# Token order restored at the eviction of y, token blocks outermost in its tile, and a new order of all compute steps, in a fused gated-recurrence and bilinear-FFN kernel

## The chip, the cores and the metric

The kernel runs on one core of a Trainium2 chip. The metric is the device time of one execution in microseconds (us), lower being better. Times are given as the median of several runs; the profile is of one execution, and its span reaches from that execution's first instruction to its last. The engines are named as the profile names them: PE (matmuls; PEld is its loading of weights), DVE (vector engine), ACT (scalar engine), POOL (GpSimd) and SP (which here only issues DMAs). POOL issues DMAs too. A source line of the kernel is written L919.

## The reference

Four batches, eight heads, 768 tokens, head dimension 48 (all inputs are float32). A gated linear-attention recurrence runs over the tokens, its output is laid out as 3072 tokens of 384 features, and a bilinear feed-forward network follows.

```python
def _attn_ref(q, k, v, alpha):
    B, H, S, D = q.shape
    state = np.zeros((B, H, D, D), dtype=np.float32)
    y = np.zeros_like(q)
    for t in range(S):
        state = alpha[:, :, t, :, None] * state + np.einsum('bhd,bhe->bhde', k[:, :, t], v[:, :, t])
        y[:, :, t] = np.einsum('bhd,bhde->bhe', q[:, :, t], state)
    return y

def _moe_ref(x, w_a, w_b, w_out):        # x (3072, 384), w_a and w_b (384, 1536), w_out (1536, 384)
    return (x @ w_a) * (x @ w_b) @ w_out
```

## The kernel before

**Tiling.** The work is cut into six chunks. Chunk c takes 256 consecutive tokens (number c//2 of the three such pieces of the sequence) of two batches (0 and 1 for even c, 2 and 3 for odd c); its two batches are called u = 0 and 1. The state of the recurrence passes from chunk c to chunk c+2. A load puts token pairs on the 128 partitions: partition p of `a`, `k`, `q`, `v` holds tokens 2p and 2p+1 of the 256, told apart by an index r. Partitions 0 to 63 and 64 to 127 are two blocks of 128 tokens each, called g = 0 and 1. So within a block the kernel's own order of columns is (r, s): the 64 even tokens, then the 64 odd ones. A block pair (u, g) makes four token blocks of 128 in a chunk, numbered 2u + g.

**Recurrence part of a chunk.** ACT takes logarithms of alpha (step `ln`, L556). Sums of pairs (`l2` on DVE, `l2s` on POOL) and triangular matmuls on PE (`B`, `A2`, `AQ`) give cumulative logs, and ACT exponentiates them (`E`, L667). DVE multiplies k and q by those factors into the tile `QKp` (`mk`, `mq`, L678). The scaled k and q are transposed into `kqT`, in chunks 0 and 1 by PE (`C`, L736) with copies out of PSUM (`Ce`), in later chunks by a DMA transpose that SP issues (`T`, L767). `dr` and `dl` (SP's DMAs through DRAM) or `dk` and `de` (PE and ACT) bring the decay factors of the state to where they are needed. `v` (L785 on ACT, L787 on DVE) casts v. `K`/`K2` are the state's matmuls on PE, `k` the state update on DVE. `D` (L841) computes scores k·q per head on PE in tiles of 64x64. They are masked either by DVE in one step (`M`, L846), or copied by ACT (`Mc`, L850) and then multiplied in place by DVE (`Mm`, L854). y is summed in PSUM from the part carried by the state (`SB`, `SA`) and the part within the block (`Y`; all three record L865).

**y's eviction.** `X u e` copies the 768 columns of both blocks of a batch from PSUM into `xT`, the transposed input of the network, on engine e (S: ACT, L900; V: DVE, L902). There are 12. `xT` is `[128, KT, B, C]`: on 128 partitions the three feature tiles, and in each the four token blocks of 128 columns. The columns keep the order (r, s).

**Network part of a chunk.** `a f w bank` and `b f w bank` (L919) multiply `xT` by 128 columns (feature block f of 12) of w_a or w_b: three matmuls that add up in one PSUM bank. With w = `*` they take all four token blocks (512 columns), with w = 0 or 1 the two blocks of one batch (256 columns). ACT copies a to SBUF (`as`, L925), DVE multiplies it by b, in PSUM, into `prod` (`pr`, L933). This product puts the tokens in natural order: it writes through `tokens`, which steps over every second element, and reads through `columns`. `o m half bank` (L941) does six of the twelve output matmuls of one token block (384 columns each), `oc` (L952) the same for half the columns in the last block of the last chunk; `ot`/`otc` (L956 on ACT, L958 on DVE) evict them, and `st`/`stc` store them by DMA (`Y` after a `st` or `ld` is SP, `P` is POOL).

**Weights.** `W a lo hi` and `W b lo hi` (L529) load columns lo to hi of w_a and w_b, `Wo` (L532) loads w_out, all issued by POOL between its other work, as are most loads of chunks 0 to 2.

**The order.** Nothing is reordered by a scheduler. A string, `PROGRAM` (lines 17 to 401), lists every step of every chunk in the order in which it is issued, chunk number first; a table `OPS` maps a step's name to a function. Each engine takes its own steps in that order, and semaphores hold a step until its operands are there and its buffer or PSUM bank is free. The last number of `a`, `b`, `o`, `D`, `SB` and the like is one of eight PSUM banks (`D` and `SB` take two). So the place of a step in the string sets what stands ahead of it in its engine's queue. In the list, chunks overlap: the recurrence steps of chunk c+1 stand among the network steps of chunk c.

Of the kernel before, what the change touches and what calls it, by code (L numbers as in the profile page):

```python
# [130 lines left out]
2: mq 0 V
1: b 3 1 3; b 0 0 6; as 3 1; as 0 0; b 0 1 7; pr 3 1; a 8 0 1; a 9 0 5
0: st 1 Y
1: b 8 0 3; b 9 0 4; pr 0 0; as 0 1
2: mk 0 V
1: a 4 1 2
3: ln *
1: a 9 1 6; pr 0 1; as 8 0; b 9 1 1
3: ra 1
1: b 10 1 7; pr 8 0; a 10 1 3; as 4 1; as 9 0; as 9 1; a 6 1 6; b 6 1 2; b 11 1 5; pr 4 1; as 10 1; pr 9 0; a 11 1 4; pr 10 1; pr 9 1; as 6 1  # L140
2: v 1 S
1: a 8 1 3; b 8 1 1; a 7 1 6; pr 6 1
3: l2 0 V
1: as 11 1
2: T 0
1: as 8 1; a 5 1 4
3: ra 0
1: as 5 1; a 1 1 2
2: v 0 V
4: ld a * Y  # L150
1: pr 11 1; as 7 1; pr 8 1
2: K2 * * 0 7; D 1 1 3; D 1 0 5
1: as 1 1; b 5 1 2; o 2 0 1
2: k * 0 V
1: pr 5 1
3: v 0 S; v 1 S
1: b 1 1 2
2: Mc 1 0; M 1 1
3: l2s 0 P; l2s 1 P
1: b 7 1 0; o 2 1 -; pr 1 1; o 3 0 4  # L160
2: SB 0 5
1: pr 7 1
3: R 0
2: D 0 0 2
1: ot 2 V
2: Mm 1 0 V
# [12 lines left out]
2: Y 1; SA 1; Mm 0 1 V; Mm 0 0 V; Y 0; X 0 S
3: E 0 b  # L180
4: l2 0 V
2: X 1 V
1: o 0 1 -
2: b 1 * 6; a 1 * 5
3: E 1 b
4: ld k * Y
3: E 1 i
1: ot 0 S
3: E 0 i
4: l2s 0 P  # L190
2: a 0 * 0; b 0 * 1; as 0 *; as 1 *
3: lv 0 k P; lv 0 q P
2: a 5 * 7
1: st 3 Y
2: a 7 * 4
4: l2s 1 P
2: a 2 * 5
3: lv 1 q V; mq 1 V; lv 1 k V
2: pr 1 *
3: dr  # L200
2: pr 0 *
3: mk 0 V
4: ld q * Y
0: st 2 Y
2: as 5 *; a 6 * 6; b 6 * 2; as 7 *
3: mq 0 V
2: b 9 * 4; b 7 * 0
1: st 2 Y
3: dl
4: R 0  # L210
2: b 5 * 7
1: o 1 0 3
2: a 9 * 1; pr 7 *; as 6 *
3: T 0
2: pr 6 *
4: ra 0
2: pr 5 *; a 11 * 6
3: mk 1 V
2: as 9 *; a 3 * 0
4: lv 0 k V; lv 0 q V; R 1  # L220
2: as 2 *
1: o 1 1 -
2: as 11 *; a 8 * 5; b 11 * 2; a 4 * 7; b 2 * 1
3: T 1
1: ot 1 V
2: pr 9 *; as 8 *; pr 11 *; pr 2 *; b 8 * 3; b 4 * 5; as 4 *
# [872 lines left out]
```

## Time and profile before

| | |
|---|---|
| time, median of 3 runs | 194.18 us (193.73 to 194.41) |
| span of the profiled execution | 192.0 us (its whole time is not recorded apart from the span) |
| `a` and `b` matmuls, L919 | 540, busy 112.0 us |
| output matmuls, L941 | 276, busy 49.4 us |
| score matmuls, L841, and y's, L865 | 384 and 576, busy 9.0 and 10.5 us |
| products, L933, on DVE | 90 |
| y evictions, L900 and L902 | 9 on ACT and 3 on DVE, busy 7.2 and 2.9 us |
| DMA | 29.40 MB, 153 GB/s on average |
| granted TensorE clock | 1.000 |

A row such as "L919 ... x270 | 56.0, 337" gives a group of instructions, their number, their busy time in all and the mean duration of one in ns. Matmuls are pipelined, so their durations overlap, and the mean of one is longer than the time by which each moves the next: with 512 columns they follow each other in less than the 337 ns that the mean shows. In the row of slices, PE is busy at 90% or more in all but the first and the last of the 40 slices of 4.8 us:

```profile
PE   7999999999999999999999999999999999999992
DVE  2387698994989888899897956887567446252510
ACT  4448885656779867753487756743572435314211
PEclk9999999999999999999999999999999999999999
GB/s 132 274 219 218 251 253 235 244 269 264 251 107 166 165 216 265 248 254 149 233 213 181 156 174 129 3 42 140 146 66 44 85 0 0 0 0 3 164 82 82
```

DVE and ACT are busiest in the first two thirds, where recurrence and network steps overlap, and little in the last fifth. The transfers are over, but for the last stores, by about 154 us.

### The profile page before, as it was taken

The numbers are of one execution on the slowest core, as the hardware profiler recorded it, in microseconds if no ns is written. First come the engines' busy times: TensorE is split into PE (matmuls) and PEld (weight loads), VectorE is DVE, ScalarE is ACT, GpSimd is POOL, SyncE is SP. The second block draws the span as 40 slices with busy tenths as digits, with TensorE's granted clock in tenths as the row PEclk, the third lists the DMA queues.
The fourth block names the chain that finished last, engine by engine and source line by source line (L and its number), as shares of the span: only waits on it lengthen the run. The fifth ranks groups of instructions, "written<-read, shape, count | busy, mean of one in ns | idle before, by whom it ended". The sixth has DMA issues, their size and how long they took to land.

```text
span 192.0 us, 6086 instructions
## 1 busy us (share of the span) xinstructions
PE 186.8 (97%) x2613; PEld 116.9 (61%) x2613; DVE 133.1 (69%) x223; ACT 106.5 (55%) x194; POOL 56.9 (30%) x75
## 2 busy tenths in 40 slices
PE   7999999999999999999999999999999999999992
PEld 3888875677778876645557444656465644545562
DVE  2387698994989888899897956887567446252510
ACT  4448885656779867753487756743572435314211
POOL 8999626752450500640074262000000000000000
PEclk9999999999999999999999999999999999999999
DMA  5999999999969999999999989017641200000422
GB/s 132 274 219 218 251 253 235 244 269 264 251 107 166 165 216 265 248 254 149 233 213 181 156 174 129 3 42 140 146 66 44 85 0 0 0 0 3 164 82 82
DMA packets 62618, 29.40 MB, mean 153 GB/s; under 512 B 53712, under 2 KB 60768, under 8 KB 62592
## 3 DMA queue, kind: packets, MB, share of 16 engines
q0 software_dynamic: 18432, 13.37, 39.6%
q1 hardware_dynamic: 44016, 15.55, 38.1%
q8 instruction: 20, 0.33, 0.7%
q10 hardware_dynamic: 144, 0.10, 0.2%
q14 instruction: 6, 0.05, 0.1%
HBM read 25.98 MB, written 4.74 MB: 160 GB/s over the span
## 4 chain that ended last, share of the span: by engine, by line
PE 91%; DMA 5%; SPq 1%; DVE 1%; issue 1%; ACT 0%; DVEq 0%
PE psum L919 47%; PE psum L941 24%; PE psum L865 7%; PE psum L841 3%; DMA kqT<-QKp 3%; DMA q_t<-in_q_dram 3%; PE psum L736 2%; PE psum L633 1%; PE psum L952 1%; SPq L549 1%; PE psum L799 1%; PE psum L812 1%; PE psum L700 1%; PE psum L591 1%; PE psum L592 1%
## 5 line engine op out<-in xcount | busy, mean ns | idle before, releaser
L919 PE MATMUL psum<-xT,wb_t 128*128 128x512 bf16 (+1 forms) x270 | 56.0, 337 | 0.0
L919 PE MATMUL psum<-xT,wa_t 128*128 128x512 bf16 (+1 forms) x270 | 56.0, 337 | 0.0
L941 PE MATMUL psum<-wo_t,prod 128*128 128x384 bf16 x276 | 49.4, 326 | 0.0
L919 PEld LDWEIGHTS <-wb_t 128*128 128x128 bf16 x270 | 25.9, 98 | 19.9 <-issue 0.5
L919 PEld LDWEIGHTS <-wa_t 128*128 128x128 bf16 x270 | 25.9, 98 | 19.7 <-issue 0.3
L941 PEld LDWEIGHTS <-prod 128*128 128x128 bf16 x276 | 25.9, 98 | 17.6
L956 ACT ACTIVATE ot<-psum 128x384 f32<-128x384 f32 (+1 forms) x16 | 7.7, 482 | 22.7 <-PE psum L941 21.6
L850 ACT ACTIVATE m<-psum 128x1024 bf16<-128x1024 f32 x14 | 14.1, 1023 | 4.6 <-PE psum L841 4.3
L613 POOL TENSOR_TENSOR l<-la 64x384 f32<-64x384 f32 x7 | 7.8, 1108 | 26.6 <-ACT la L556 19.0
L846 DVE TENSOR_TENSOR m<-psum,mask 128x1024 bf16<-128x1024 f32 x10 | 12.1, 1220 | 3.1 <-PE psum L841 3.1
L652 POOL TENSOR_TENSOR q_t<-q_t,ra 128x384 f32<-128x384 f32 x5 | 6.1, 1215 | 22.5 <-ACT ra L645 19.7
L556 ACT ACTIVATE la<-a_t 128x1536 f32<-128x1536 f32 (+2 forms) x9 | 9.5, 1055 | 2.3 <-DMA a_t<-in_alpha_dram 2.2
L678 DVE TENSOR_TENSOR QKp<-q_t,beta 128x768 bf16<-128x768 f32 x10 | 10.0, 995 | 1.0 <-ACT beta L667 1.0
L865 PE MATMUL psum<-m,vx 64*64 64x128 bf16 x576 | 10.5, 217 | 0.0
L900 ACT ACTIVATE xT<-psum 128x768 bf16<-128x768 f32 x9 | 7.2, 816 | 5.7 <-PE psum L865 5.5
L678 DVE TENSOR_TENSOR QKp<-k_t,invb 128x768 bf16<-128x768 f32 x10 | 9.7, 972 | 0.8 <-ACT invb L667 0.8
L854 DVE TENSOR_TENSOR m<-m,mask 128x1024 bf16<-128x1024 bf16 x14 | 9.3, 684 | 1.2 <-ACT m L850 1.2
L958 DVE COPY ot<-psum 128x384 f32<-128x384 f32 (+1 forms) x9 | 4.8, 532 | 7.6 <-PE psum L941 4.7
L865 PEld LDWEIGHTS <-vx 64*64 64x64 bf16 x576 | 9.0, 107 | 0.5 <-issue 0.3
L841 PE MATMUL psum<-kqT 64*64 64x128 bf16 x384 | 9.0, 219 | 0.4 <-DMA kqT<-QKp 0.3
L652 POOL TENSOR_TENSOR k_t<-k_t,a_t 128x384 f32<-128x384 f32 x6 | 7.4, 1228 | 6.1 <-issue 3.3
L549 POOL DMA_DIRECT2D v_t<-in_v_dram x8 | 8.5, 1058 | 0.1
(271 smaller groups left out, 287.9 us busy)
## 6 DMA issues: line engine op xcount, KB each, us to landing
out_dram<-ot SPq DMA_DIRECT2D x23, 192.0 KB, 3.8
q_t<-in_q_dram SPq DMA_DIRECT2D x3, 768.0 KB, 6.5
a_t<-in_alpha_dram POOLq DMA_DIRECT2D x2, 768.0 KB, 15.2
k_t<-in_k_dram POOLq DMA_DIRECT2D x2, 768.0 KB, 12.1
v_t<-in_v_dram POOLq DMA_DIRECT2D x4, 384.0 KB, 7.0
a_t<-in_alpha_dram SPq DMA_DIRECT2D x2, 768.0 KB
k_t<-in_k_dram SPq DMA_DIRECT2D x2, 768.0 KB
a_t<-in_alpha_dram POOLq DMA_DIRECT2D x3, 384.0 KB, 8.5
```

The costliest lines, as they stand in the source:

```text
L549: eng.dma_start(out=t[:, us, hs].rearrange("p b h r d -> p (b h) (r d)"), in_=src[ch.b0 + us.start:ch.b0 + us.stop, hs, ch.s * 2 * C:(ch.s ...
L556: nc.scalar.activation(out=ch.la[:, us, hs].rearrange("p b h r d -> p (b h r d)"), in_=ch.a[:, us, hs].rearrange("p b h r d -> p (b h r d) ...
L613: eng.tensor_add(ch.l2[(1 - g) * HC:(2 - g) * HC, 1], x[:, :, 0, :], x[:, :, 1, :])
L652: eng.tensor_mul(x, x, by)
L678: eng.tensor_mul(QKp[ch.c % 2][:, u, j, :, hs, :D], src[:, u, hs].rearrange("p h r d -> p r h d"), f)
L841: nc.tensor.matmul(s2[g * HC:(g + 1) * HC, r, p, rk, :], lhsT=turned_part(ch, u, 1, rk, 2 * h + p, g, rs), rhs=queriesT(ch, u, 2 * h + p, ...
L846: nc.vector.tensor_mul(m.rearrange("p r a k s -> p (r a) (k s)"), ch.s2[u, h].rearrange("p r a k s -> p (r a) (k s)"), maskn(4))
L850: nc.scalar.activation(out=m.rearrange("p r a k s -> p (r a) (k s)"), in_=ch.s2[u, h].rearrange("p r a k s -> p (r a) (k s)"), func=AF.Copy)
L854: eng.tensor_mul(x, x, maskn(4))
L865: nc.tensor.matmul(y[c * DP:(c + 1) * DP, g, j // 2 * C:(j // 2 + 1) * C], lhsT=lhsT, rhs=rhs, start=(g, c) not in begun, stop=False, skip ...
L919: nc.tensor.matmul(p, lhsT=(wa_t, wb_t)[w][:, kk, f * 128:(f + 1) * 128], rhs=ch.xT[:, kk, us, :], start=(kk == 0), stop=(kk == KT - 1))
L941: nc.tensor.matmul(op, lhsT=ch.prod[:, f, at:at + C], rhs=wo_t[:, f, :], start=(f == 0), stop=(f == NFF - 1))
```

## The change

`xT` becomes `[128, B, KT, C]`: token blocks outermost, the three feature tiles within. `X u e` becomes `X u g e`: one block (384 columns) is evicted at a time, so there are 24 evictions instead of 12, of half the size each. 17 are on ACT and 7 on DVE. The eviction now writes the columns in natural token order: its output steps over every second element. So `pr` reads and writes plain runs, and the helpers `tokens` and `columns` are gone. A matmul `a` or `b` reads, for feature tile kk, one run of 128 columns out of each token block, 384 columns apart, where it read one run of 512 or 256.

The string `PROGRAM` is replaced. The steps are the same in kind, number and width (90 `a`, 90 `b`, 46 `o`, 4 `oc`), but for `X`. All compute steps stand in new places, with new PSUM banks. POOL's steps stand in the same sequence, and so do the loads that SP issues; SP's stores and its `dr`, `dl` and `T` have moved among those loads in places. Four `v` casts move from ACT to DVE, and three `ot` evictions move from ACT to DVE. The first program lines (up to the first network steps), the places where chunk 4's logarithms and chunk 2's masking stand, and the end are shown in full below; the rest of the string is left out.

```diff
 PROGRAM = """
-0: cm 0; c1; cz 0 b P; ci; ld a 0b Y; c1a; ld a 0a Y; ln 0b; cu; cz 1 b P; fill 7 2; cu2 V; cz 0 q V; cus; ld k 0b Y; ld k 0a Y; B 0b 5; ld q 0b Y; ld v 0 P
-0: ln 0a; ld q 0a Y; E 0b b; E 0b i; mq 0b V; B 0a 0; E 0a i; dk 0 2; E 0a b; ld a 1 P; mk 0b V; C 0 1 5; cs 0 m P; ld k 1 P; ld q 1 P; v 0 S; mk 0a V; cm 1
-0: de 0; fill 2 1; mq 0a V; C 0 0 3; Ce 0 1 V; W b 0 256; cz 0 v P; Ce 0 0 V; D 0 1 4; ln 1; ld v 1 P; W a 256 768; K 0 0 6; k 0 0 V; M 0 1; D 0 0 0; SB 0 6
-0: cz 1 q P; B 1a 2; M 0 0; W a 0 256; E 1a i; E 1a b; W b 256 768; mq 1a V; mk 1a V; B 1b 4; dk 1 3; E 1b i; E 1b b; de 1; v 1 S; mq 1b V; mk 1b V; C 1 0 0
-0: Y 0; SA 0; Ce 1 0 V; cs 1 m P
-1: ld a 0 P; ld a 1 P
-0: W a 768 1536; C 1 1 1; X 0 S; c2 P; D 1 0 3; W b 768 1536
-1: ld q 0 P
-0: Ce 1 1 V; K 1 0 5; k 1 0 V; a 4 0 0
-1: ld k 0 P
-0: D 1 1 6; SB 1 1
-1: ld v 0 P; ld q 1 P
-0: Mc 1 0; a 3 0 5; Wo 0 6; a 0 0 3; Mm 1 0 V; Mc 1 1; as 0 0; b 0 0 4
-1: ld k 1 P
-0: pr 0 0; b 1 0 6; a 2 0 3; a 1 0 7; a 5 0 4; as 2 0; b 2 0 3; Mm 1 1 V; as 1 0; b 4 0 7; as 5 0; b 5 0 4; pr 2 0; pr 1 0
-1: ln 0
-0: SA 1; Y 1; Wo 6 12; K 1 1 6; as 3 0; as 4 0; X 1 S
...
+0: ld a 0b Y; c1a; c1; cm 0; ld a 0a Y; cz 0 b P; fill 7 0; ln 0b; ci; cu; cu2 V; cus; ln 0a; B 0b 2; cz 1 b P; ld k 0b Y; B 0a 0; dk 0 4
+0: ld k 0a Y; E 0b i; mk 0b V; ld q 0b Y; cz 0 q V; ld v 0 P; E 0b b; mq 0b V; C 0 1 5; fill 2 2; ld q 0a Y; E 0a b; mq 0a V; E 0a i; mk 0a V; ld a 1 P; C 0 0 0; v 0 V
+0: K 0 0 1; cs 0 m P; ld k 1 P; Ce 0 0 V; Ce 0 1 S; de 0; D 0 1 2; ld q 1 P; k 0 0 V; D 0 0 4; cm 1; M 0 1; W b 0 256; M 0 0; SB 0 0; ln 1; B 1a 6; E 1a i
+0: B 1b 2; dk 1 4; cz 0 v P; mk 1a V; E 1a b; mq 1a V; C 1 0 5; ld v 1 P; E 1b i; mk 1b V; E 1b b; de 1; W a 256 768; Y 0; SA 0; X 0 1 S; cz 1 q P; mq 1b V
+0: C 1 1 4; X 0 0 S; Ce 1 0 V; D 1 0 2; Mc 1 0; v 1 V; K 1 0 5; K 0 1 1; Ce 1 1 V; D 1 1 6; k 1 0 V; SB 1 4; W a 0 256; a 1 0 0; as 1 0; a 3 0 2; k 0 1 V; b 1 0 3
+0: pr 1 0; as 3 0; Mm 1 0 V; W b 256 768; a 0 0 0; b 3 0 1; Mc 1 1; Mm 1 1 V; cs 1 m P; pr 3 0; as 0 0; b 4 0 2; b 5 0 3; a 5 0 0; as 5 0; a 2 0 6; K 1 1 7; k 1 1 V
+0: Y 1
+1: ld a 0 P
+0: SA 1; X 1 0 V; a 4 0 0; b 0 0 1
...
+0: X 1 1 S; b 2 1 4
+1: ln 1; l2 1 V
+0: b 3 1 1; as 4 0; pr 4 0; a 2 1 5
 1: H 1 V
...
+0: as 2 1; pr 2 1; a 3 1 0; as 3 1; pr 3 1; W a 768 1536; a 7 * 3; as 2 0; a 6 * 0; a 9 * 2; c2 P; as 9 *; a 1 1 6; b 5 1 1; W b 768 1536
+1: ra 0; A2 0 4; E 0 i; E 0 b; L 1 V
+0: pr 2 0; b 9 * 2; pr 9 *; a 5 1 7
...
-2: Mc 0 1
-4: ln *
...
+4: ln *
+3: R 0
+2: Mc 0 1
+0: cs 0 0 P
+1: o 3 0 1; o 3 1 -
+3: R 1; AQ 6; E 1 b; E 1 i; E 0 b
+2: SA 0
...
-5: ot 0 V; o 2 1 -; oc 1 0 1 -; otc 1 0 V; ot 3 S; oc 1 1 0 0; st 0 Y; st 3 Y; ot 2 S; st 2 Y; oc 1 1 1 -; otc 1 1 S; stc 1 1 S; stc 1 0 Y
+5: o 0 0 0; pr 6 *; pr 8 *; o 3 0 1; o 3 1 -; o 2 0 2; o 2 1 -; ot 3 V; ot 2 V; o 0 1 -; ot 0 S; st 0 Y; st 3 Y; st 2 Y; oc 1 1 0 1; oc 1 1 1 -; otc 1 1 V; stc 1 1 S
+5: oc 1 0 0 0; oc 1 0 1 -; otc 1 0 S; stc 1 0 Y
 """
...
-    def evac(ch, u, eng):
+    def evac(ch, u, g, eng):
         if not hasattr(ch, "xT"):
-            ch.xT = wk.tile([128, KT, B, C], BF16, name="xT")
-        o_ = ch.xT[:, :, 2 * u:2 * u + 2, :].rearrange("p a g s -> p g a s")
-        i_ = ch.y[u][0][:, :, :KT * C].rearrange("p g (a s) -> p g a s", a=KT)
-        if eng is nc.scalar:
-            nc.scalar.activation(out=o_, in_=i_, func=AF.Copy)
-        else:
-            eng.tensor_copy(o_, i_)
+            ch.xT = wk.tile([128, B, KT, C], BF16, name="xT")
+        evict(ch.xT[:, 2 * u + g].rearrange("p a (s r) -> p a r s", r=2),
+              ch.y[u][0][:, g, :KT * C].rearrange("p (a r s) -> p a r s", a=KT, r=2), eng)
...
-    def tokens(x, us):
-        return x.rearrange("p (b s r) -> p b r s", s=HC, r=2)[:, us]
-
-    def columns(x, n):
-        return x.rearrange("p (b r s) -> p b r s", r=2, s=HC)
...
-            nc.tensor.matmul(p, lhsT=(wa_t, wb_t)[w][:, kk, f * 128:(f + 1) * 128], rhs=ch.xT[:, kk, us, :], start=(kk == 0), stop=(kk == KT - 1))
+            nc.tensor.matmul(p, lhsT=(wa_t, wb_t)[w][:, kk, f * 128:(f + 1) * 128], rhs=ch.xT[:, us, kk, :], start=(kk == 0), stop=(kk == KT - 1))
...
-        o_, a_, b_ = tokens(ch.prod[:, f, :], us), columns(a[:, :n], n), columns(b, n)
-        nc.vector.tensor_mul(o_, a_, b_)
+        nc.vector.tensor_mul(ch.prod[:, f, us.start * C:us.stop * C], a[:, :n], b)
...
-        "X": lambda x, u, e: evac(x, int(u), ENG[e]),
+        "X": lambda x, u, g, e: evac(x, int(u), int(g), ENG[e]),
```

`evict`, which the new `evac` calls, is the function that output evictions use already: on ACT an activation with the copy function, on DVE a copy.

More of the change, by code (lines that the diff above doesn't have):

```diff
@@ new lines @@
+2: K2 * * 5 3; D 0 0 6
+1: pr 9 1
+2: k * 0 V
+3: ld q * Y
+1: o 2 0 0
+3: l2 0 V
+1: b 6 1 1; b 4 1 2
+2: Mc 0 0; k * 1 V
+1: a 10 1 5; b 10 1 6
+3: ld k * Y
+1: a 6 1 7; o 2 1 -; as 4 1; pr 4 1
+3: v 0 S
+2: SB 0 2
+1: as 10 1; pr 10 1; as 6 1; pr 6 1
+3: l2s 1 P
+2: SB 1 4; D 0 1 6
+4: ln *
[5 more added lines that the diff above has]
+2: SA 0
+4: ld k * Y
+3: E 0 i
+2: Mm 0 1 V; Mm 0 0 V; Y 0; Y 1; SA 1; X 1 1 S
+1: o 0 0 7; o 0 1 -
+2: X 0 0 V
+0: st 1 Y
@@ new lines @@
+3: SA 1
+4: E 0 b; E 0 i
+1: st 0 Y
+4: E 1 i
+3: Mm 0 0 V; Y 0; Mm 1 1 V; Y 1; X 1 1 S; SA 0; X 0 1 S
+2: o 3 0 1; o 1 0 3
+3: X 1 0 S; X 0 0 V; b 8 * 2; a 3 * 4; a 1 * 5; a 8 * 6
+5: l2s 1 V
+4: lv 0 q V; mk 0 V; ld v * P; v 0 S
+3: as 8 *; a 9 * 7
+2: o 1 1 -
+4: mq 0 V; T 0
+5: ld k * P; l2 0 V; l2s 0 P; R 0; ra 0
+4: mk 1 V
+3: pr 8 *; as 1 *; as 3 *
+2: o 3 1 -
+3: b 1 * 2; pr 1 *
+2: ot 2 S; st 2 Y
+4: mq 1 V
+3: a 6 * 0; b 3 * 6; b 6 * 2
+4: D 0 0 4
+3: as 6 *
+1: st 1 Y
+3: b 9 * 0
+5: lv 0 k P
@@ new lines @@
+4: dr
+2: ot 1 V
+3: pr 3 *
+2: st 1 Y
+5: ra 1; lv 1 q P
+4: T 1; dl
+3: as 9 *
+5: R 1
+2: o 0 0 3; o 0 1 -
+3: pr 6 *; a 11 * 2
+2: ot 3 V; st 3 Y
+3: a 0 * 1; as 0 *; a 5 * 6
+4: M 0 0; v 1 V
+3: a 2 * 7; b 0 * 1
+5: ld v * P
+3: as 2 *; b 2 * 4; pr 9 *; as 11 *; pr 0 *; pr 2 *; b 5 * 7; b 11 * 2; as 5 *; pr 5 *
+2: ot 0 S
+4: D 1 0 0
+3: pr 11 *
+4: D 0 1 4; Mc 1 0; D 1 1 6; Mc 1 1; K * 0 3
+5: lv 1 k P
+4: M 0 1
+3: a 4 * 2; as 4 *; a 7 * 0; as 7 *
+5: v 0 S
+4: k * 0 V
+3: a 10 * 1
+4: SB 0 2; SB 1 4
@@ new lines @@
+5: D 0 0 4; D 0 1 6; Mc 0 0; K * 0 0; T 1; D 1 1 2; Mc 1 1
+4: a 4 * 1; as 4 *
+5: dl
+3: st 2 Y
+5: k * 0 V; M 0 1
+3: o 3 0 4; o 3 1 -; ot 3 V
+4: a 9 * 0
+5: Mm 0 0 V
+4: as 9 *; b 1 * 1; pr 1 *
+5: SB 1 2; SB 0 4; D 1 0 6; M 1 0
+3: o 1 0 0; o 1 1 -
+5: Mm 1 1 V
+4: a 8 * 1; b 9 * 6
+5: SA 1; Y 1; X 1 0 V; X 1 1 S; SA 0
+4: as 8 *
+5: Y 0
+4: a 7 * 7; b 8 * 1
+5: X 0 1 V; X 0 0 S; a 1 * 2
+4: pr 9 *
+5: a 4 * 3
+4: pr 8 *
+3: ot 1 S
+4: b 4 * 6
+5: b 10 * 0
+4: pr 4 *; a 10 * 1
+5: a 10 * 6; a 7 * 4; as 10 *; pr 10 *; as 1 *; b 1 * 5; pr 1 *
@@ L401 @@
+4: o 1 0 4; o 1 1 -; o 3 1 -; st 0 Y
+5: a 8 * 0; pr 2 *; b 6 * 2
+4: o 2 0 3; o 2 1 -
+5: as 8 *
+4: ot 3 V; st 3 Y; ot 1 S; st 1 Y; ot 2 S; st 2 Y
+5: o 0 0 0; pr 6 *; pr 8 *; o 3 0 1; o 3 1 -; o 2 0 2; o 2 1 -; ot 3 V; ot 2 V; o 0 1 -; ot 0 S; st 0 Y; st 3 Y; st 2 Y; oc 1 1 0 1; oc 1 1 1 -; otc 1 1 V; stc 1 1 S
+5: oc 1 0 0 0; oc 1 0 1 -; otc 1 0 S; stc 1 0 Y
 """
```

491 lines of the change are left out of this document (160 added, 331 removed).

## The prediction

> **What bounds the kernel now.** I read the page's busy shares first, then the chain that ended last, then what PE waited for.
>
> ```profile
> PE 186.8 (97%) x2613; PEld 116.9 (61%) x2613; DVE 133.1 (69%) x223; ACT 106.5 (55%) x194; POOL 56.9 (30%) x75
> PE 91%; DMA 5%; SPq 1%; DVE 1%; issue 1%; ACT 0%; DVEq 0%
> PE psum L574 <- DVE og L472: 1.2, 1, 1.2
> PE psum L841 <- DMA kqT<-QKp: 0.3, 1, 0.3
> PE psum L736 <- DVE QKp L678: 0.2, 1, 0.2
> ```
>
> PE is busy nearly throughout and ends the chain, and everything that it waited for is three waits, two of them in the first 9 us. Busy alone proves little, since matmuls overlap, so I take their pace from the pieces of the chain in order of time (start, length, what):
>
> ```profile
> 51.03 0.97 PE psum L941 x6
> 57.47 9.93 PE psum L919 x90
> 74.77 1.08 PE psum L941 x6
> 106.47 4.99 DMA kqT<-QKp
> 111.92 9.17 PE psum L919 x42
> 187.17 1.50 PE psum L952 x18
> 188.69 0.33 ACT ot L956
> ```
>
> A 256-column matmul takes 9.93/90 = 110 ns, a 512-column one 9.17/42 = 218, an output one (384 columns) 163. The six at 74.77 follow 64x64 matmuls and take 0.1 more: a switch between whole array and 64x64 tiles costs about 0.1. With these prices I keep a ledger of PE's work in program order: at the first `a` step (18.32 us) the clock is 6.7 us ahead of the work done, at 107 us 6.4, at the end 6.6. So after 18 us almost nothing is lost: 0.3 at 24.6 (the matmuls behind `X 1 S`) and 0.4 at 111 (the transposed tile above). All that better placing can win is the first 18 us, those 0.7, and the 3.4 from the last matmul (188.66) to the end of the span (192.0).
>
> **The change part by part.** *Matmuls.* Each kind of step has the same count and width on both sides (90 `a`, 90 `b`, of each 54 at 512 columns, 36 at 256; 46 `o`, 4 `oc`); the switches go from 55 to 54: -0.1. The moving tile of `a` and `b` is now read in runs of 128 columns, 384 apart, where it was one run. Bounds: L633, whose moving operand steps over every second element, does four 384-column matmuls per 0.16 us, its full rate, so nothing; at the other end L591 (f32) needs 163 ns for 192 columns, twice the pace. I take nothing: L841 reads two runs of 64, near to this, sixteen in 0.22 us. Advanced Engine Details and Errata (Memory Cachelines) of the Trainium skill speaks against the change if read on the moving operand: any non-contiguous access pattern is said to slow matmuls significantly (said of PSUM); L841 and L633 do not bear it out for SBUF.
>
> *Evictions and products.*
>
> ```profile
> L900 ACT ACTIVATE xT<-psum 128x768 bf16<-128x768 f32 x9 | 7.2, 816 | 5.7 <-PE psum L865 5.5
> L956 ACT ACTIVATE ot<-psum 128x384 f32<-128x384 f32 (+1 forms) x16 | 7.7, 482 | 22.7 <-PE psum L941 21.6
> L902 DVE CAST xT<-psum 128x768 bf16<-128x768 f32 x3 | 2.9, 952 | 2.4 <-PE psum L865 2.4
> L958 DVE COPY ot<-psum 128x384 f32<-128x384 f32 (+1 forms) x9 | 4.8, 532 | 7.6 <-PE psum L941 4.7
> 159.50 0.73 DVE L933 TENSOR_TENSOR prod<-as__3200,psum 128x512 bf16<-128x512 bf16 x1 [3.23 <-PE psum L919]
> 160.12 0.71 DVE L933 TENSOR_TENSOR prod<-as__3202,psum 128x512 bf16<-128x512 bf16 x1
> ```
>
> Twelve evictions of 768 become 24 of 384. ACT: 17 x 0.49 = 8.3 for 7.3; DVE: 7 x 0.55 = 3.9 for 2.9. They now write every second element; the products did that so far, at 0.62 start to start (159.50 to 160.12), and a mask multiply with contiguous output (L846, 1,134 ns start to start for 1,024) scales to 0.60. So a strided write costs 0 to 0.04 on either engine, and the 54 wide products save 54 x 0.02 = 1.1 (bounds 0 to 2.3). With `v` (four from ACT's 0.85 to DVE's 0.35) and three `ot` moved to DVE, DVE gets some 3 us more and ACT 4 less: DVE stays near 70% of the span, under PE. Of this only the way from `Y` to the first `a` is on PE's path: two halves on two engines end 0.49 to 0.56 after `SA` or `Y` instead of 0.82, so the 0.3 at 24.6 goes.
>
> *Start.* GpSimd's and SP's loads stand in the same order, so landings should stay. DVE now does `mk 0b` while the q load is still under way and `cz 0 q` behind it; it is free for `mq 0b` at about 8.1, 0.3 behind that load's landing (7.7). `C 0 1` then starts near 8.7 (8.94 before). `Ce 0 1` goes to ACT (1.02 instead of 0.70), beside `C 0 0` and `Ce 0 0`. The next hold is the second alpha load, landed at 10.8 in both; `B 1a` starts behind `SB 0` and `ln 1` (11.64) at 11.7 instead of 12.0. Walking on with the same durations, `C 1 0` comes at 15.2 (15.7) and the first `a` at 18.6 with 0.66 us more work done before it: 0.4 ahead in the ledger (6.3). Bounds 0 to 0.6.
>
> *Weights.* What comes next on PE is new: `b 3 0` third but one, `a 7 *` before most of chunk 0's half steps.
>
> ```profile
> 12.86 0.77 POOL L529 DMA_DIRECT2D wb_t<-in_moe_w_b_dram  x1
> 15.64 0.77 POOL L529 DMA_DIRECT2D wa_t<-in_moe_w_a_dram  x1
> wa_t<-in_moe_w_a_dram POOLq DMA_DIRECT2D x1, 576.0 KB, 10.3
> wb_t<-in_moe_w_b_dram POOLq DMA_DIRECT2D x1, 384.0 KB, 7.6
> 26.91 0.81 PE L919 MATMUL psum<-xT,wa_t 128*128 128x512 bf16 x3
> ```
>
> Columns 256 to 767 of w_b land at 12.86 + 7.57 = 20.4, columns 768 on of w_a at 15.64 + 10.3 = 25.95. Before, the first use of the latter came at 26.91, a us late enough. Now `b 3 0 1` is reached at 19.9 and waits 0.5 (ledger 6.9); `a 7 *`, 6.5 us of work after the first `a`, is reached at 25.6 and waits 0.3 (ledger 7.2, where before stood at 7.0). `b 9 *` (landing 16.97 + 11.87 = 28.84) comes at 28.9. The start's gain is eaten: +0.2 at 26 us, between -0.7 (weights a us earlier) and +0.6.
>
> *Middle.* For each `a`, `b`, `o`, `D`, `SB`, `Y` I summed the work queued on ACT or DVE ahead of what frees its bank or makes its operand. The tightest are `a 9 *` behind `pr 4 0`, `b 9 *`, `b 5 1` (0.1 each), `C 0 0` of chunk 1 (0.2), `D 0 0` of chunk 2 behind its transpose (0.3, at the longest seen from issue to landing, 5.9); the rest have 0.3 and more. Three or four can cost 0.1: +0.2 (0 to 2). The 0.4 at 111 goes: chunk 4's `T 0` to `D 0 0` has a us to spare. On SP `st 0` now stands ahead of chunk 2's `dr` and `T 1`, its result copied some 10 us earlier; `st 1` moved behind the chunk 3 and 4 loads.
>
> *End.* The last half store goes out through SP instead of ACT. Three stores of 192 KB are issued in the last 1.4 us of PE instead of 3.8. Four stores at 180 moved 360 KB/us, so 688 KB need 1.9 from 0.7 behind the first issue: done 1.2 after PE, before the last half store can start (1.1 to 1.2; before 1.1). Zero, between -0.1 and +0.5.
>
> *Sum:* +0.2 (weights) - 0.4 (transpose) - 0.1 (switch) + 0.2 (thin margins) + 0 = -0.1 on a span of 192.0. The profiled execution's whole time is not shown apart; the median of the runs, 194.18, lies 2.2 over its span (1.7 to 2.4). 191.9 + 2.1 = **194.0 us**.
>
> **Rivals.**
> *ACT is held by a load (slower).* Chunk 4's `ln *` now stands on ACT ahead of chunk 2's `Mc 0 1`, on which `Mm 0 1` and both `Y` hang; before it stood behind. Its alpha load is issued on SP behind chunk 2's `T 0`. Before: issue 66.26, and with the 6.5 of such loads landed by 72.8, `ln` at 75.6 without a wait. Now `ln` is due near 73.5. For: the margin falls from 2.8 to 0.7 us. Against: `T 0` is issued a us earlier. Each us of landing past 73.5 is a us of PE; at 2 to 3, 196.5. Chance 0.12.
> *Thin margins add up (slower).* Waits of 0.1 to 0.3 at ten of some 300 places, and weights 0.5 later: +1.2, 195.3. For: every place is recomputed by sums, not seen. Against: the same sums give the old order within 0.3. Chance 0.22.
> *The runs of xT slow PE (slower).* At half pace 324 x 216 + 216 x 109 ns = +93 us, 287 us; a tenth of that, 203. Chance 0.03; the skill's sentence on non-contiguous patterns is this rival.
> *The start's gain stays (faster).* Weights land 0.5 to 1 earlier, because landings move with traffic: -0.5 - 0.4 - 0.1 = -1.0, 193.2. Against: queue order and bytes are the same. Chance 0.27.
>
> **How the numbers follow.** A measurement of this kernel can tell about 0.3% (0.6 us) from no change. The likeliest, no change within that, has 0.36 (193.6 to 194.8 alone); faster 0.27; slower 0.12 + 0.22 + 0.03 = 0.37. The range 192.9 to 196.6 takes in the faster rival down to half a us under its value and the first two slower ones; outside are the third and tails, under 2 in 10.
>
> **What would show it.** Right: first `a` matmul near 18.6, PE waits on wb_t near 20 and on wa_t near 26, no PE wait on kqT at 111, L919 at 216 and 109 ns start to start, ACT evictions at 0.49, PE's last matmul near 188.5. Wrong: PE waiting for DVE or ACT between 30 and 180 us by more than 0.5 in all, L919 wider than 0.22, or `ln` of chunk 4 waiting for a_t.

## The result, and the profile after

The changed kernel takes 198.71 us (median of 4 runs, 198.2 to 200.48) where the kernel before took 194.3 (4 runs, 193.73 to 194.62): slower by a factor of 1.0248, 95% interval 1.0201 to 1.0294. The prediction was 194.0, with a range of 192.9 to 196.6. The time lies outside it: next to no change was forecast (-0.1 us), and the kernel is 4.4 us slower.

The profiled execution of the new kernel took 200.48 us, with a span of 198.7; it is the slowest of the four. The spans of the other three were 196.4 to 197.2. So its trace shows some 2 us more than a usual run, and the text says where these are.

From the new kernel's page, the busy shares, the granted clock by slices of 4.97 us and the engines' shares of the chain that ended last:

```profile
PE 189.1 (95%) x2612; PEld 116.6 (59%) x2613; DVE 138.3 (70%) x234; ACT 101.5 (51%) x195; POOL 57.5 (29%) x75
...
PEclk9999999999999999999999699999999999999999
...
PE 63%; DMA 15%; DVE 7%; POOL 5%; issue 3%; ACT 2%; SPq 2%; POOLq 0%; DVEq 0%; ACTq 0%
```

Shares alone look much as before (DVE 70 for 69%, ACT 51 for 55). What differs is the chain: PE made up 91% of it and now makes up 63, and DMA has gone from 5 to 15%. One slice of the clock row, the one that begins at 109.3 us, is at 6 tenths. PE's waits (line, what it waited for, us in total, times, longest):

```profile
PE psum L862 <- ACT xT L877: 2.3, 1, 2.3
...
PE psum L668 <- DVE QKp L610: 0.6, 1, 0.6
PE psum L841 <- DVE ot L879: 0.5, 1, 0.5
PE psum L841 <- DVE ll L539: 0.5, 1, 0.5
```

The longest is new: at 107.5 us PE stands for 2.3 us, for an eviction of y. ACT's own order there, first before and then after (start, length, instruction, and in brackets the idle time ahead of it and what ended it):

```profile
99.14 1.48 ACT L556 ACTIVATE la<-a_t 128x1536 f32<-128x1536 f32 x1
...
104.76 1.54 ACT L900 ACTIVATE xT<-psum 128x768 bf16<-128x768 f32 x2
```

```profile
101.57 1.02 ACT L782 ACTIVATE m<-psum 128x1024 bf16<-128x1024 f32 x1 [0.21 <-PE psum L773]
106.22 1.48 ACT L488 ACTIVATE la<-a_t 128x1536 f32<-128x1536 f32 x1 [3.63 <-DMA a_t<-in_alpha_dram]
107.61 0.85 ACT L599 ACTIVATE beta<-psum 128x384 f32<-128x384 f32 x2
...
109.10 1.52 ACT L877 ACTIVATE xT<-psum 128x384 bf16<-128x384 f32 x3
```

ACT reached chunk 5's logarithms (`5: ln *`) at 102.6 and stood for 3.6 us, until alpha had landed at 106.2; behind them stood the exponentials of chunk 4 and the three evictions of chunk 3 that PE needed. Before, the same step ran at 99.14 without a wait. SP had issued that load at 91.25 before and at 94.10 after, so it took under 7.9 us then and 12.1 now:

```profile
85.61 5.54 SPq L767 DMA_TRANSPOSE kqT<-QKp  x2
91.25 0.96 SPq L549 DMA_DIRECT2D a_t<-in_alpha_dram  x1
```

```profile
87.21 6.79 SPq L699 DMA_TRANSPOSE kqT<-QKp  x2
94.10 0.53 SPq L481 DMA_DIRECT2D a_t<-in_alpha_dram  x1
```

The other transfers of that stretch are POOL's. Its sequence is the same, but not its times. Before:

```profile
97.16 1.00 POOL L652 TENSOR_TENSOR q_t<-q_t,ra 128x384 f32<-128x384 f32 x1 [13.30 <-ACT ra L645]
...
99.37 1.20 POOL L549 DMA_DIRECT2D v_t<-in_v_dram  x1
100.57 1.17 POOL L549 DMA_DIRECT2D k_t<-in_k_dram  x1
```

After:

```profile
89.28 1.00 POOL L584 TENSOR_TENSOR q_t<-q_t,ra 128x384 f32<-128x384 f32 x1 [5.38 <-ACT ra L577]
...
91.18 1.21 POOL L481 DMA_DIRECT2D v_t<-in_v_dram  x1
92.37 1.17 POOL L481 DMA_DIRECT2D k_t<-in_k_dram  x1
```

In both, POOL waits for ACT's step `4: ra 1`. In the new order this step runs 8 us earlier (at 88.61 instead of 96.51), so POOL's v load of chunk 4 (384 KB) and k load of chunk 5 (768 KB) go out at 91 to 92 instead of 99 to 101: among chunk 3's two transposes and ahead of the alpha load, where they used to go out behind it.

After the 2.3 us of idle PE the clock fell. Two stretches of the new kernel (length, PE's busy time with its instructions, granted clock, DMA share, GB/s):

```profile
110.70:115.00 4.30, 4.30 (x14) 0.60 0.42 80
115.00:118.00 3.00, 3.00 (x18) 1.00 0.36 69
```

4.3 us at 0.60 of the clock lose 4.3 x 0.4 = 1.7 us (within that stretch the clock is at 0.50 for 3.4 us and at 1.00 around it). The other three runs had a mean clock of 0.997 to 1.000 (this one 0.991), so this loss belongs to the profiled run and not to the median.

The prediction's ledger (PE's clock minus the work done, by the same prices), read again in both traces, places the whole difference. Each row names the state of both kernels at about that time:

| at | before | after |
|---|---|---|
| first `a` step (18.3; 19.2) | 6.7 | 6.9 |
| behind the first steps on the last weights (27 us) | 7.0 | 8.0 |
| 56 us | 6.8 | 8.7 |
| 82 us, behind the wait for `ot` | 6.7 | 9.1 |
| 95 us | 6.6 | 9.3 |
| behind the wait for `xT` (107; 110.7) | 6.4 | 12.1 |
| behind the slow clock (115 us) | 6.8 | 13.8 |
| end | 6.6 | 13.6 |

The columns lie 1.0 us apart at 27 us, 1.7 more at 95, 3.0 more behind the wait for `xT`, and 1.3 more behind the slow clock (1.7, less the 0.4 that the old order loses at 111 us). That is 7.0 in all, for spans that differ by 6.7; the medians differ by 4.4 only. In this execution the held ACT is the largest part, the clock belongs to it, and the rest is spread over the weights and some six small places. Another trace of the same order, under "The eviction's stride", shows a usual run, and there ACT is held far less.

### The profile page after: what moved, and what is told of

Its sections match the earlier page's. It is cut to its first block, busy times and chain, and to the rows that moved or that the text cites. A ratio compares the mean times of both kernels' runs of the same rounds, so it can differ in the third digit from the quotient of the medians.

```text
span 198.7 us, 6085 instructions
## 1 busy us (share of the span) xinstructions
PE 189.1 (95%) x2612; PEld 116.6 (59%) x2613; DVE 138.3 (70%) x234; ACT 101.5 (51%) x195; POOL 57.5 (29%) x75
## 4 chain that ended last, share of the span: by engine, by line
PE 63%; DMA 15%; DVE 7%; POOL 5%; issue 3%; ACT 2%; SPq 2%; POOLq 0%; DVEq 0%; ACTq 0%
PE psum L841 38%; PE psum L862 16%; DMA q_t<-in_q_dram 6%; DMA k_t<-in_k_dram 5%; DMA wb_t<-in_moe_w_b_dram 4%; PE psum L797 4%; SPq L481 2%; PE psum L773 1%; DVE prod L854 1%; PE psum L873 1%; POOL v_t L481 1%; DVE QKp L610 1%; PE psum L744 1%; POOL wa_t L461 1%; PE psum L731 1%
## 5 line engine op out<-in xcount | busy, mean ns | idle before, releaser
L841 PE MATMUL psum<-xT,wa_t 128*128 128x512 bf16 (+1 forms) x270 | 57.5, 342 | 1.0 <-DVE ot L879 0.5
L841 PE MATMUL psum<-xT,wb_t 128*128 128x512 bf16 (+1 forms) x270 | 56.6, 339 | 0.2
L862 PE MATMUL psum<-wo_t,prod 128*128 128x384 bf16 x276 | 48.7, 326 | 2.3 <-ACT xT L877 2.3
L841 PEld LDWEIGHTS <-wa_t 128*128 128x128 bf16 x270 | 25.9, 99 | 21.4 <-issue 3.1
L862 PEld LDWEIGHTS <-prod 128*128 128x128 bf16 x276 | 26.1, 98 | 20.7 <-issue 2.5
L841 PEld LDWEIGHTS <-wb_t 128*128 128x128 bf16 x270 | 25.8, 98 | 20.7 <-issue 0.9
L545 POOL TENSOR_TENSOR l<-la 64x384 f32<-64x384 f32 x7 | 8.6, 1226 | 37.3 <-ACT la L488 14.3
L877 ACT ACTIVATE ot<-psum 128x384 f32<-128x384 f32 (+1 forms) x13 | 6.2, 480 | 15.1 <-PE psum L862 13.6
L879 DVE COPY ot<-psum 128x384 f32<-128x384 f32 (+1 forms) x12 | 6.5, 538 | 10.6 <-PE psum L862 8.3
L877 ACT ACTIVATE xT<-psum 128x384 bf16<-128x384 f32 x17 | 9.1, 607 | 8.4 <-PE psum L797 8.3
L610 DVE TENSOR_TENSOR QKp<-k_t,invb 128x768 bf16<-128x768 f32 x10 | 11.7, 1174 | 0.9 <-issue 0.6
L778 DVE TENSOR_TENSOR m<-psum,mask 128x1024 bf16<-128x1024 f32 x10 | 12.1, 1217 | 0.0
L797 PE MATMUL psum<-m,vx 64*64 64x128 bf16 x576 | 10.3, 217 | 0.3 <-issue 0.3
L786 DVE TENSOR_TENSOR m<-m,mask 128x1024 bf16<-128x1024 bf16 x14 | 10.0, 744 | 0.7 <-ACT m L782 0.6
L610 DVE TENSOR_TENSOR QKp<-q_t,beta 128x768 bf16<-128x768 f32 x10 | 10.3, 1032 | 0.2
L773 PEld LDWEIGHTS <-kqT 64*64 64x64 bf16 x384 | 6.4, 106 | 2.9 <-issue 1.3
```

Of the source, the lines that this page charges most:

```text
L545: eng.tensor_add(ch.l2[(1 - g) * HC:(2 - g) * HC, 1], x[:, :, 0, :], x[:, :, 1, :])
L610: eng.tensor_mul(QKp[ch.c % 2][:, u, j, :, hs, :D], src[:, u, hs].rearrange("p h r d -> p r h d"), f)
L773: nc.tensor.matmul(s2[g * HC:(g + 1) * HC, r, p, rk, :], lhsT=turned_part(ch, u, 1, rk, 2 * h + p, g, rs), rhs=queriesT(ch, u, 2 * h + p, ...
L778: nc.vector.tensor_mul(m.rearrange("p r a k s -> p (r a) (k s)"), ch.s2[u, h].rearrange("p r a k s -> p (r a) (k s)"), maskn(4))
L786: eng.tensor_mul(x, x, maskn(4))
L797: nc.tensor.matmul(y[c * DP:(c + 1) * DP, g, j // 2 * C:(j // 2 + 1) * C], lhsT=lhsT, rhs=rhs, start=(g, c) not in begun, stop=False, skip ...
```

## The experiments

**Theories.** *Placement:* the loss comes from waits for transfers, most of it from ACT held by chunk 5's alpha load, and that load is late because POOL's two loads were released early. *Layout:* the new `xT` (runs of 128 columns under the matmul, strided and split evictions) costs. *SP's queue:* the alpha load is late because it stands behind the transposes.

**The layout alone.** The old order with the new layout:

```diff
-X 0 S
+X 0 0 S; X 0 1 S
```

(and so for all twelve, each half on its old engine).

> The old order of steps with the new layout: each eviction of y is split in two at its old place and on its old engine. If the loss comes from the new order (waits for loads), this runs like the kernel before: 194.3 us, within 0.6, with no PE wait after 25 us longer than 0.4. If the layout itself costs (runs of 128 columns under the matmuls, strided and split evictions), most of the 4.4 us is here: 197 to 199 us, and the 512-column matmul takes more than 216 ns from start to start.

It took 194.03 us (10 runs), the kernel before 194.27 (13 runs): ratio 1.0001, interval 0.9984 to 1.0018. Its matmuls on `xT`, from the list of groups (count, busy us, mean ns):

```profile
L909 PE MATMUL psum<-xT,wa_t 128*128 128x512 bf16 (+1 forms) x270 | 56.0, 337 | 0.4 <-ACT xT L945 0.4
```

56.0 us and 337 ns are what the kernel before has. The layout costs nothing that these runs can tell (under 0.4 us by the interval), so the loss is in the order.

**The held step moved.** The new kernel with chunk 5's logarithms behind chunk 3's evictions:

```diff
-5: ln *
 4: R 1
...
-5: l2s 1 V
+5: ln *; l2s 1 V
 4: lv 0 q V; mk 0 V; ld v * P; v 0 S
```

> The new kernel with chunk 5's logarithms moved behind chunk 3's four evictions of y on ACT; nothing else. If ACT, held by chunk 5's alpha load ahead of these evictions, is what stops PE at 108 us, the wait of 2.3 us goes, and with it the slower clock behind it (1.7 us in the profiled run): 195.0 to 196.7 us. If something else is as late (chunk 4's scaled k and q, which DVE makes behind the sums of those logarithms), less than 1 us is gained: 197.7 to 198.7 us.

It took 202.32 us, 3.6 more than the new kernel and above both expected ranges. The evictions were no longer behind the logarithms, but the logarithms now stood behind the evictions: they ran at 108.65 instead of 106.22, without a wait for the load. DVE's `l2s` waits for the same logarithms, and behind it stand the scalings for chunk 4 and the product that frees a PSUM bank. PE's longest wait in that run:

```profile
PE psum L840 <- DVE prod L853: 2.9, 1, 2.9
```

Two queues hang on these logarithms, and what one gains by the move the other pays. The run does not show why the load is late; the next one tests that. (This run also waited 1.6 us for w_b near 21 us, on which more below.)

**The release moved back.** The new kernel, the one step `4: ra 1` later on ACT:

```diff
-4: ra 1
 5: ld a * Y
...
-4: lv 1 q P
+4: ra 1; lv 1 q P
```

> The new kernel with one step of chunk 4 (the ratio that releases POOL's scaling of q and k, and behind it POOL's v load of chunk 4 and k load of chunk 5) moved some 9 us later on ACT; the logarithms stay. If the alpha load of chunk 5 is slow because those two loads go out 2 to 3 us ahead of it, it lands 4 to 5 us earlier (near 101 instead of 106.2), ACT is not held, and the time is 195.0 to 196.7 us. If it is late because it stands behind the two transposes in SP's queue, it lands at 105 to 106 as before and the time stays at 198 to 199 us.

It took 196.39 us (196.18 to 196.53), ratio to the kernel before 1.0130 (1.0105 to 1.0156): 2.3 of the 4.4 us are gone. POOL's v load went out at 100.7. SP issued the alpha load at 93.42, behind the transposes as in the new kernel, and the logarithms found it landed:

```profile
101.60 1.02 ACT L781 ACTIVATE m<-psum 128x1024 bf16<-128x1024 f32 x1 [0.21 <-PE psum L772]
102.52 1.48 ACT L487 ACTIVATE la<-a_t 128x1536 f32<-128x1536 f32 x1
```

The load took at most 9.1 us instead of 12.1. Its place in SP's queue, which is the same, is not the cause.

**The load moved ahead of the transposes.**

```diff
+5: ld a * Y
 3: lv 1 q V; T 0; mq 1 V
...
-5: ld a * Y
 4: l2s 1 P
```

> The new kernel with the alpha load of chunk 5 moved ahead of chunk 3's two transposes in SP's queue; nothing else. It is issued near 86 instead of 94.1 us. Under both explanations of its lateness (traffic of the v and k loads, or the place behind the transposes) it lands by about 97 and ACT is not held: 195.0 to 196.7 us. If the transposes, now behind it, come too late for chunk 3's scores, PE waits for them near 94 us instead, by 1 to 3 us, and the time stays at 197 to 199 us.

It took 202.42 us, more than either case had it. The alpha load, issued at 86.89, landed at 93.9, and the logarithms had no wait. But the transposes, now with three loads beside them, came late. SP's row for both was 6.79 us long in the new kernel and is 12.35 here, and PE waited for the tile:

```profile
87.94 12.35 SPq L699 DMA_TRANSPOSE kqT<-QKp  x2
```

```profile
PE psum L773 <- DMA kqT<-QKp: 4.6, 1, 4.6
```

**The early release alone, in the old kernel.**

```diff
-4: ra 0
+4: ra 0; ra 1
...
-4: ra 1
```

> The old kernel with one step moved: chunk 4's second ratio on ACT stands behind the first, some 11 us earlier (85 instead of 96.5 us), as in the new order. If the release of POOL's two loads is what hurts, they now go out near 88 to 90 us, ahead of chunk 5's alpha load (91.3), which lands 3 to 5 us later (102 to 104 instead of before 99); its logarithms, due at 99.1, hold ACT ahead of chunk 3's evictions, and the time is 196 to 199 us. If it takes the rest of the new order for that, the time is that of the kernel before, 194.3 us within 0.6.

One small step, moved 11 us forward on an engine with time to spare, made the old kernel 12 us slower: 206.31 us, ratio 1.0601 (1.0568 to 1.0634). POOL's loads went out at 88.4 and 89.8. The alpha load landed only at 111.8, 16.9 us after its issue, as the theory has it; but PE had long been stopped by something else, the second transposed tile of chunk 3, issued at 89.45:

```profile
108.73 1.06 PE L840 MATMUL psum<-kqT 64*64 64x128 bf16 x32 [10.92 <-DMA kqT<-QKp]
```

While PE stood, the transfers moved 95 GB/s (windows of that run; DMA share and GB/s stand last):

```profile
98.00:108.70 10.70, 0.00 (x0) 0.00 (x0) 0.45 (x1) 0.51 (x1) 0.00 (x0) 0.70 1.25 95
108.70:113.00 4.30, 4.27 (x44) 2.37 (x44) 3.03 (x4) 2.24 (x2) 0.00 (x0) 0.57 1.29 261
```

I read this as loads that slow the transposes beside them and the loads behind them; the gate below tests it. The size was mis-expected (196 to 199), since I had counted only with the alpha load.

**Only the loads held back.** Does the early release hurt by the two loads, or by POOL's scaling, which it brings forward too? A gate on POOL (a copy of one element of the transposed tile) lets the scaling run early and holds the loads until the second transposed tile is there. In the new kernel and in the old one with the early release:

```diff
+3: gatet 1
 4: ld v * P
```

> The new kernel with the ratio in its new, early place, so that POOL scales q and k early too; but POOL then waits for chunk 3's second transposed tile before it issues the v and k loads (one element of the tile is copied). If those two loads, started among the transposes and ahead of the alpha load, are what delays the alpha load, it lands by 101 to 102 as with the late ratio and the time is 195.9 to 196.9 us. If it was POOL's scaling that hurt (DVE slowed beside it) or something else that comes with the early ratio, the time stays at 198 to 199 us.

> The old kernel with the early ratio (206.3 us) and the same gate on POOL. If transposes and loads that run at once slow each other, the 12 us go and the time is 194.0 to 195.2 us. If the scaling on POOL, or its being 11 us earlier, is what cost 12 us, it stays above 200 us.

The new kernel with the gate took 196.31 us (ratio 1.0112, 1.0082 to 1.0142), the same as with the late release. The old kernel with the early release and the gate took 194.09 (ratio 1.0020, 0.9995 to 1.0045): all 12 us are gone. In that run the gate opened at 93.75, and the logarithms ran at their old time:

```profile
93.75 0.18 POOL L993 CAST go<-kqT 1x1 f32<-1x1 bf16 x1 [5.35 <-DMA kqT<-QKp]
94.43 1.21 POOL L549 DMA_DIRECT2D v_t<-in_v_dram  x1 [0.49 <-issue]
```

```profile
98.99 1.48 ACT L556 ACTIVATE la<-a_t 128x1536 f32<-128x1536 f32 x1
```

So the cost is that of the two loads going out early, shown in both orders. The gate holds them behind the transposes and behind the alpha load alike, so it does not tell by which of these they cost.

**The eviction's stride.** The new kernel writing plain runs, for the duration alone (it leaves out the return to natural token order, so the rows of its output stand in the kernel's own order):

```diff
-evict(ch.xT[:, 2 * u + g].rearrange("p a (s r) -> p a r s", r=2), ...)
+evict(ch.xT[:, 2 * u + g], ...)
```

> The new kernel with the eviction of y writing plain runs, so that the tokens stay in the kernel's own order and the rows of the output come out permuted; the rest is the same. If the step over every second element is what makes an eviction on ACT take 0.61 us instead of the 0.49 of an output eviction of the same size, it takes 0.49 here; if it is the type or the row of PSUM, 0.6. On DVE 0.55 to 0.59 either way. The time stays that of the new kernel within 1 us, since the evictions are not what PE waits longest for.

It took 198.51 us in its one run, as the new kernel. First the groups of the new kernel (ACT, DVE), then those of this one:

```profile
L877 ACT ACTIVATE xT<-psum 128x384 bf16<-128x384 f32 x17 | 9.1, 607 | 8.4 <-PE psum L797 8.3
L879 DVE CAST xT<-psum 128x384 bf16<-128x384 f32 x7 | 4.1, 590 | 5.6 <-PE psum L797 5.6
```

```profile
L877 ACT ACTIVATE xT<-psum 128x384 bf16<-128x384 f32 x17 | 7.5, 494 | 8.6 <-PE psum L797 8.6
L879 DVE CAST xT<-psum 128x384 bf16<-128x384 f32 x7 | 3.9, 554 | 5.6 <-PE psum L797 5.6
```

The step over every second element costs 113 ns on ACT and 36 on DVE per eviction, and no part of the loss can be seen to come from it.

This run is also a second trace of the new order, and one of usual length (span 196.7 us, clock 1.000). POOL's two loads go out as early in it (91.92 and 93.12), but PE stands in another place, and ACT hardly at all:

```profile
100.30 0.64 PE L773 MATMUL psum<-kqT 64*64 64x128 bf16 x32 [1.07 <-DMA kqT<-QKp]
```

```profile
105.58 1.48 ACT L488 ACTIVATE la<-a_t 128x1536 f32<-128x1536 f32 x1 [0.81 <-DMA a_t<-in_alpha_dram]
```

PE waits for chunk 3's transposed tiles, 1.5 us in two waits where the late release has 0.4 in one, and so reaches the later steps later; ACT stands 0.8 us for alpha instead of 3.6, and PE does not wait for an eviction of y. That the early loads cost is shown by the kernels that hold them back. That they cost by holding ACT is read from the execution profiled first; here they more likely cost by the tiles, which no run tests by itself.

**The remaining 2.1 us.** Three kernels on top of the late release tried to take the small waits of the ledger away. The first moves the output eviction that PE waited for at 82 us ahead of the step on DVE that waits for the k load:

```diff
+1: ot 3 V
 3: lv 1 k V
 4: l2s 0 P
 3: mk 1 V
-1: ot 3 V; st 3 Y
+1: st 3 Y
```

> The kernel with the late ratio (196.4 us) and one more move: the eviction of an output tile that frees a PSUM bank for chunk 2's second network step stands ahead of chunk 3's scaling of k on DVE, which waits for the k load. If the 0.6 us that PE loses there is a loss of its own: 195.6 to 196.0 us. If the next wait takes it back (the transposed tile at 93.8 us comes no earlier): 196.2 to 196.6 us.

It took 195.88 us (195.16 to 197.49), ratio 1.0091 (1.0058 to 1.0124). That is 0.5 less than with the late release alone, as expected for a loss of its own, though the two intervals overlap.

The second adds three moves: in chunk 0 `a 1 1 6; b 5 1 1` ahead of `a 7 * 3; as 2 0`, chunk 3's `D 0 0 6; Mc 0 0` behind `2: a 2 * 1`, and `3: pr 8 *` ahead of `4: mk 1 V`.

> The kernel with the late ratio and four moves: that output eviction ahead of the k load's user on DVE; in chunk 0 the first steps on the last half of w_a behind two half steps (0.5 to 0.6 us of other work first); chunk 3's first scores behind one step of chunk 2 (0.4 us, the transposed tile); the product that frees a bank at 113 us ahead of a scaling of k on DVE (0.3 us). If the remaining 2.1 us over the kernel before are these small waits, each its own: 194.3 to 195.0 us. If each is passed on to the next: 195.5 to 196.4 us.

It took 198.8 us, above both expected ranges. The move in chunk 0 was a bad one: `b 5 1 1` needs the bank that `pr 3 1` frees, and PE waited 2.1 us for that product. In this kernel `a 1 1` also overwrites a bank that `as 2 0` had yet to read, so part of chunk 0's product has a wrong factor; the work is the same in amount. The third leaves that move out:

> The new order with the late ratio and three moves, without the one in chunk 0: the output eviction ahead of the k load's user, chunk 3's first scores behind one step of chunk 2, and the product that frees a bank at 113 us ahead of a scaling of k. If the remaining waits after 80 us are each their own: 195.0 to 195.6 us. If they are passed on: 195.9 to 196.4 us.

It took 197.58 us (195.94 to 197.89, five runs), ratio 1.0158 (1.0120 to 1.0196): above both expected ranges, and not better but 1.7 worse than without the two moves at 95 and 113 us. In the traces of this kernel and of the first (there of its slowest run, 197.49) PE waits 1.7 us for a transposed tile of chunk 4 near 126 us, and 1.5 and 1.6 us for w_b near 21. The late release alone, in its trace, has neither wait. The w_b wait lies ahead of every moved step, so the moves did not make it. The tile wait may be time taken out at one place and lost to the next transfer, but no run tests that, and how often either wait comes is not known.

**The old order mended.** The old order with the new layout and three moves against its three small waits:

```diff
-as 3 0; as 4 0; X 1 0 S; X 1 1 S
+as 4 0; as 3 0; X 1 0 S; X 1 1 V
...
-4: D 0 0 3
...
-4: v 1 S; M 0 0
-3: b 1 * 7; as 1 *;
+4: v 1 S
+3: b 1 * 7
+4: D 0 0 3; M 0 0
+3: as 1 *;
```

> The old order with the new layout (194.0 us) and three moves. In chunk 0 the second half of batch 1's eviction goes to DVE, beside ACT's, and two copies on ACT change places: the waits of 0.2 and 0.4 us at 24 to 25 us should go. Chunk 4's first scores stand behind one more network step: the wait of 0.4 us at 111 us for the transposed tile should go. If these waits are each their own: 193.0 to 193.5 us. If later waits take the time back (w_a's last half lands at 26.5 and is used at 27.6; evictions and transfers behind): 193.8 to 194.3 us.

It took 194.51 us, the kernel before beside it 193.85: ratio 1.0040 (1.0021 to 1.0058), so slower, and above both expected ranges. By the ledger the waits at 24 and 111 us are gone, and 0.4 us each was lost right behind them. No version tried here beats the kernel before.

## Why the prediction was wrong, point by point

**The step that failed** is "GpSimd's and SP's loads stand in the same order, so landings should stay". The order did stay, but a load goes out when its engine gets to it, and POOL is let through by ACT's `ra` steps. The one that counts, `4: ra 1`, had moved by 8 us, and I did not follow it. In the sums for the middle of the kernel every operand load then had its old landing time. Holding the two loads back again took 2.3 to 2.4 of the 4.4 us away. Neither the wait of 3.6 us on ACT in the profiled execution nor the 1.1 us on chunk 3's second tile in the other trace was in any sum, though the trace of before had what was needed: that POOL had waited 13.3 us for `ra`, and that two loads stood right behind.

**The rival that came true**, in the profiled execution, is "ACT is held by a load", at a chance of 0.12. It was put on chunk 4's logarithms. Those waited 0.2 us at 73.3: that margin was sized well. Chunk 5's logarithms, by the same mechanism, were not looked at. The rival's rule, that each us of landing past the due time is a us of PE, held roughly: 3.6 us past 102.6 made 2.8 in the ledger, and the price at 2 to 3 us, 196.5, fell short because other terms were too small as well. In the other trace of this order ACT is held 0.8 us, and PE does not wait for the evictions. So the rival had the right kind of cause, a late load, on the wrong chunk, and on a path that not every run takes.

**The clock** was in no sum: 1.7 us in the profiled run.

**Start.** The first `a` was to come at 18.6 with the ledger at 6.3; it came at 19.2 with 6.9. `B 1a` started at 11.99 and not at 11.7, since the second alpha load landed at 11.07 instead of 10.8. In the other traces of the study that load landed between 10.3 and 11.1, so a gain of 0.3 that hangs on it was not to be had for sure. The gain of 0.4 became a loss of 0.2.

**Weights.** The mechanism was right and the size half: PE waited for w_b at 20.7 (0.25) and for the last half of w_a at 26.7, which landed at 26.69 instead of 25.95. (The list of waits puts the latter down to `ll`, L539, which ended at the same moment; PE's weight load there was waiting for w_a.) The ledger stood at 8.0 where 7.2 was forecast.

**Middle.** "+0.2 (0 to 2)" for the thin margins was too low, though its bounds held: 1.3 came between 27 and 95 us (8.0 to 9.3), of it 0.7 behind `ot 3`, which stood on DVE behind a step that waited for chunk 3's k load. Again it was a load, and not the work ahead on the engine. The wait for chunk 4's tile at 111 us did go.

**Right:** matmuls at 216 ns on the new `xT` and no cost of the layout; the sentence of Advanced Engine Details and Errata of the Trainium skill (Memory Cachelines) on non-contiguous patterns, weighed as a rival at 0.03, is not borne out for the moving operand in SBUF (ratio 1.0001). Products: 683 ns for 725, start to start 598 for 620, the 0.02 that was taken. The end: PE's last matmul to the end of the span 3.2 us, before 3.4. **Mis-sized:** evictions on ACT, 0.49 taken and 0.61 measured, off PE's path but for one place. And the whole time was taken as 2.1 us over the span, where every run recorded has 1.7 to 1.9.

**Open.** Of the 4.4 us in the medians 2.3 are shown to be the two loads, and 0.5 is likely the eviction behind the k load. The other 1.6 I read from the ledger of one execution (the weights in the first 27 us, thin margins after) without an experiment that took them away.

## What to carry to other kernels

That an engine's sequence is copied does not mean that its transfers start when they did: for each load, find the instruction ahead of it that waits, and what releases that. A step that comes earlier on an engine with time to spare can start a transfer that slows those on the path. When a step held by a load stops a queue, ask first why the load is late: here moving the step only made the next queue that needs the same data wait.

## What the runs showed of the hardware that I had not expected

**Transposes and loads slow each other.** SP's row for a pair of DMA transposes was 5.5 us long where POOL's loads came later (old order; 6.2 in the new order with the late release), 6.8 and 9.0 where they ran beside them, and 12.4 with a third load ahead. In the worst case a tile landed some 19 us after its issue, and the core's transfers fell to 95 GB/s. DMA: Bandwidth & Descriptors of the Trainium skill (Rules for kernel authors) says that a transpose next to ordinary DMAs needs nothing; that is said of whether the data come out right, and it says nothing of the time, which is what grew here.

**A short wait can lower the clock.** Behind a wait of 2.3 us the granted clock was 0.60 for 4.3 us; waits of 2.1 us and less (mean clock of those runs 1.000) left it alone, and behind 10.9 us it was 0.57. The runs with waits of 2.9 and 4.6 us had a mean clock of 0.991 and 0.983. TensorE: Matmul & The Clock Gate of the Trainium skill (What's actually happening) has the clock halve after an idle window of some 3.4 us; here 2.3 us was enough in one run.

**DVE and POOL hold each other up.** Beside POOL's scaling, DVE's scaling of k took 1.57 us, where the kernel before has a mean of 0.97:

```profile
79.80 1.57 DVE L610 TENSOR_TENSOR QKp<-k_t,invb 128x768 bf16<-128x768 f32 x1
```

```profile
79.20 1.35 POOL L584 TENSOR_TENSOR k_t<-k_t,a_t 128x384 f32<-128x384 f32 x1 [1.29 <-DMA k_t<-in_k_dram]
```

It also works the other way, and goes with when weights land. POOL's mask step ahead of the w_b load takes 0.42 us or up to 1.29. First the new kernel, then the one with the moved output eviction, where DVE's two scalings ran without a gap (from 7.99 to 9.17):

```profile
7.49 0.42 POOL L434 TENSOR_SCALAR_AFFINE_SELECT mask<-mask 64x256 bf16<-64x256 bf16 x1
...
8.51 0.76 POOL L461 DMA_DIRECT2D wb_t<-in_moe_w_b_dram  x1
```

```profile
7.48 1.28 POOL L434 TENSOR_SCALAR_AFFINE_SELECT mask<-mask 64x256 bf16<-64x256 bf16 x1
...
9.36 0.84 POOL L461 DMA_DIRECT2D wb_t<-in_moe_w_b_dram  x1
```

The w_b load behind it is then issued 0.85 us later, and in that run PE waited 1.6 us for w_b's columns 256 to 767 (`PE psum L841 <- DMA wb_t<-in_moe_w_b_dram: 1.6, 1, 1.6`). In the nine traces of the new order and its variants the two go together: in the three where the mask step took 1.07 us or more PE waited 1.5 or 1.6 us for these columns, in the six with 0.82 or less at most 0.3. SBUF — State Buffer of the Trainium skill (Who interferes with whom) states a lock between a DVE instruction with two SBUF inputs and a GpSimd instruction that reads SBUF. Both observations agree with it; that the lock is the cause was not tested by itself.
